# 64 small identity products in TensorE's program, and an opening re-ordered around them, in a delta-rule attention and MLP kernel

## The chip, the cores and the metric

One core of a Trainium2 chip. The metric is the device time of one execution in microseconds; several runs of the same kernel are given by their median. Lower is better.

## What is computed

Four sequences, eight heads, 768 tokens, 48 features per head, all fp32. The attention block runs the delta rule token by token; its output, 3072 x 384, goes through an MLP with 2048 hidden units and a hard swish.

```python
k_n = k / (norm(k, axis=-1) + 1e-06)
state = zeros((B, H, D, D))
for t in range(S):
    y[:, :, t] = einsum('bhd,bhde->bhe', q[:, :, t], state)
    v_old = einsum('bhde,bhd->bhe', state, k_n[:, :, t])
    state = state + beta[:, :, t] * einsum('bhd,bhe->bhde', k_n[:, :, t], v[:, :, t] - v_old)
x = y.transpose(0, 2, 1, 3).reshape(B * S, H * D)
h = x @ w_in
out = (h * clip(h + 3, 0, 6) / 6) @ w_out
```

The inputs also hold weights in a 64-bit type, which the kernel converts on the chip.

## The kernel before

**Chunks.** Tokens are taken in 24 chunks of 32 for all four sequences at once (128 partitions). Within a chunk the recurrence is solved in closed form: a lower triangular system of 32 unknowns per head and sequence is inverted. Chunk 0 is inverted by a chain of small products (`product`); chunks 1 to 4 (group 1) are inverted together on VectorE by elimination of the two 16 x 16 halves (`halves_of`: a transposition L469, pairs of steps L730 and L735, a transposition back L473), and then each of these chunks joins its two halves by two products on TensorE (`join`, L684 with the names pi1 and pi2). Later groups are inverted wholly on VectorE.

**What a chunk needs, step by step.** `prep`: the keys are scaled on GpSimd (kb, L510), keys and queries are turned by four transpositions each on TensorE (pt, L524), and ScalarE sets the results aside (KQ, L532); TensorE then forms the products of keys and queries (sc, L547), and VectorE masks them into L and LB (L558). `chain`: the products with the state (ks, L806), R on VectorE (L901, L909), the product with the inverse (pz, L827), set aside by ScalarE (R, L927), the change of the state (su, L938; added by VectorE, L956), and the output: the product py (L827), set aside as y (L861 for chunk 0), turned on TensorE (yt, L873) and set aside as xT (L877). Chunk 0 needs no ks.

**The MLP.** xT of two chunks makes a block of 256 tokens. Block 0 is multiplied chunk by chunk with w_in (ph, L994; a "chunk of ph" below is one of the 16 column tiles of 128 hidden units, three products of 128 x 128). ScalarE takes a relu of each (g, L1001), VectorE multiplies (g, L1004). The down products (po) follow, and later blocks are multiplied by schemes with fewer products (L1066, L1226), which make up most of the time.

**The weights.** They arrive in 16 pieces of 768 KB through SP's queue (L331). For each piece ScalarE makes four passes (the scale steps, L356) and VectorE three (the convert steps L378, L383 and L389). Two buffers of scales alternate: the scale steps of a piece wait for the last convert step of the piece two before it. The bytes of a piece are loaded once the first passes over an earlier piece in the same place are done.

**Order.** Each engine works strictly through its own list. For the opening, the lists come from a table of words, ORDER, each of which lets one generator make its next step: `a` a scale step, `c` a convert step, `w` a weight load, `k`, `q`, `v` loads, `pN` a step of chunk N's prep, `hN` one of its chain, `yN` one of its output, `i1` a step of the elimination of group 1, `xN` a step of chunk N's product or join, `ua` a chunk of ph, `ra` its relu, `ga` its product. From chunk 5 on a planner spreads the steps.

**The opening's joint.** Before the change TensorE's list around the first join reads: nine products of ph (three chunks), ks of chunk 1, eighteen products of ph, pi1, six products of ph, pi2, three products of ph, pz of chunk 1. The first product of TensorE's program is the transposition of chunk 0's keys, which waits for GpSimd.

Of the kernel before, what the change touches and what calls it, by code (L numbers as in the profile page):

```python
# [22 lines left out]
k*2 B*3 k*2 n0 k*2 z B s*2 n0*6 k*2 q*2 n1 q n1 q w k p0 z*3 k n1*2 k*2 n1*2 z p0*2 s k p0*3 a k a  # L23
m0 a n2 m1 p0 x0*2 w q x0 n1 x0*3 c*2 n2 a k s p1*2 a s*2 k q s*2 x0 n2 k*2 c x0 n2 x0 w q a*4 q p1
n2 k*2 a x0 m2 p1 c*2 p1 n2*3 b1 q b0 s p1 x0 q w x0 n2 q*2 c*3 x0 n4 k p1 k p2*2 x0*2 a*2 c a*2 q*3
a*2 w v p3*2 q x0 q n4 p2*2 c p2 v c n4*2 a*3 z v n4 c a m3 v c p2 n4*2 q p2 k c b2 h0 c h0 w a*2 h0
p4*2 a*2 m4 p3 q*4 h0 q k w p4*2 c*5 v*2 p3 k p3*3 k*2 p4*2 v*2 p4 m6 k a w a w i1*3 k i1*7 a i1*2 a
i1*2 v i1*2 k b3 k y0 c y0*3 ua*2 ra*2 i1*3 w v ga v a*3 i1*2 ua i1 h1 i1 q w ua ra ua i1 ra*2 ga i1
k ua a*2 ra ga i1 ga ua ra ua ra i1 ga i1*4 ua ga n5 x1*2 k x1 c a ra v a*2 ga x2 k*2 ga*2 ua*2 x1
ra*2 x1*2 ua h1*2 n5 k ga c ra ga*2 h1 c y1*2 ua ra w ga ua ra x2 n5 ga y1*2 ua ra ga h1 v*3 n5*2 k  # L30
y1*2 ua a ra x2 ub*2 a n5 rb*2 h1 x3 ga c*2 v W a h2 y2 gb ub rb gb x2 gb ub*2 n5*2 b4 rb n5 x2*2 h2
gb rb gb m5 a n5*2 y2 ub rb gb v c q*2 v q*5 n5 ub n5 rb gb h2 c h2 q ub y2 h2 y2 rb ub p5 b5 rb
gb*2 a*2 x3 p5 ub y2*2 k p5*2 h2 rb h3 p5 gb h3 ub*2 q rb gb rb gb ub a x3 p6 v c x4 x3 rb gb ub p7
rb gb y3 c*2 v c p7*2 y3 v p7*2 b6 x3 q x3 ub p6 h3 a p6 c p5*2 rb gb k m7 w p6 h3 u p6 k*2 q*3 a*2
y3 a p6 c y3 v y3*2 u n9 v k q a c a c*2 u*2 ru gu w k a*2 c a*2 x4 c*2 ru p7 a gu k u a*2 p7 p6 m8
u*3 a k u*2 k h3 w ru*2 a*2 gu*2 x4 c*2 x4 k c*2 a p8 k a*2 u ru k h3 u*2 h4 ru a b8 gu k gu y4 p8*3
u h4 k*2 c q k*9 q u p8*2 x4 k ru k*2 gu k c n9 q u q*2 p8 k*2 b7 n9*2 i2 u x4 q i2*2 q ub ru gu u
rb gb i2*2 h4*2 u*2 i2 ru i2*6 y4 i2 gu i2*7 u i2 ru gu i2 u*3 ru i2*4 gu ru i2*2 v i2 c gu u*3 a u
ru c i2 u*2 i2 gu i2*3 q i2*5 y4 h4 n9 i2 e*2 n9*2 i2*4 q i2 y4 e n9 u ru i2*3 u i2 ru*2 gu h4 u n9
i2*2 u i2 e i2*6 y4 u k n9*3 u gu i2 y4 n9 i2 p9 q i2*2 gu  # L40
"""


# [1 line left out]
def kernel(  # L45
# [21 lines left out]
    nc = tc.nc  # L67
    B, H, S, D = q.shape
    DM, FF = moe_w_in.shape
    C, DP = 32, 64  # L70
# [11 lines left out]
    G0 = 1  # L82
# [12 lines left out]
    def rows(b):  # L95
        return slice(C * b, C * b + C)
# [4 lines left out]
    def group(t):  # L101
        return (0, t) if t < G0 else ((t - G0) // GS + 1, (t - G0) % GS)
# [34 lines left out]
    def needs(*what):  # L137
        assert past.issuperset(what), (what, set(what) - past)
# [70 lines left out]
    ident = const.tile([128, 128], FP32, name="ident")  # L209
# [87 lines left out]
    def pad(t):  # L297
        return [f"pad{t}"] if t < NBKB else []
# [195 lines left out]
    def scaled(t):  # L494
# [7 lines left out]
        past.add(("bkb", t))  # L502
        yield

    def prep(t, whole=True):

        g, i = group(t)
        kb, qb = kbufs[t % NKB], qbufs[t % NQB]
        needs(*([("bkb", t - NKB)] if t >= NKB else []), *(pad(t) if t < NKB and t else []))
        nc.gpsimd.tensor_tensor(  # L510
            out=kb[:, :, 0:D], in0=kfs[g][:, i],
            in1=invs.pop(t).unsqueeze(2).to_broadcast([P, H, D]), op=ALU.mult,
        )
        past.add(("kb", t))
        yield

        for j, src in enumerate((kb, qb)):
            if j == 1:
                needs(("q", t))
                past.add(("qT", t))  # L520
            ring("pm", NPM, ("pt", t, j))
            pt = psM.tile([128, NP, P], FP32, name="pt", tag=slot["pm"])
            for p in range(NP):
                nc.tensor.transpose(  # L524
                    pt[:, p, :], src[:, 2 * p : 2 * p + 2].rearrange("p e w -> p (e w)"), ident[:]
                )
            yield 1
            if j == 0:
                ring("KQ", NKQ, ("KQ", t))
                KQ = work.tile([128, NP * B // 2, 4, C], FP32, name="KQ", bufs=NKQ)  # L530
            read(("pt", t, j))
            nc.scalar.activation(  # L532
                out=KQ[:, :, 0:4:3, :] if j == 0 else KQ[:, :, 1:3, :],
                in_=pt[:].rearrange("q p (x y c) -> q (p x) y c", y=2, c=C), func=ACTF.Copy,
            )
            if whole and j == 0:
                drain(mask(t))
            yield
# [26 lines left out]
        if whole:  # L565
            drain(scaled(t))
        yield
# [98 lines left out]
    def join(t):  # L666
# [11 lines left out]
        def times(name, m, k):  # L678
            ring("pm", NPM, (name, t))
            ps = psM.tile([P, H, HC], FP32, name="pi", tag=slot["pm"])  # L680
            for h in range(H):
                for b in range(B):
                    r = slice(C * b, C * b + k)
                    nc.tensor.matmul(  # L684
                        ps[rows(b), h, :], lhsT=m[r, h, :], rhs=LT[r, h, HC:C],
                        start=True, stop=True, skip_group_check=True,
                        tile_position=(C * b, C * b),
                    )
            return ps
# [6 lines left out]
        ps = times("pi1", T, HC)  # L696
# [10 lines left out]
        ps = times("pi2", T2, C)  # L707
# [638 lines left out]
    def drain(gen):  # L1346
        for _ in gen:
            pass
# [53 lines left out]
    def early_norms(t):  # L1402
# [7 lines left out]
        a=scales(), c=rest, w=pieces(), q=queries(), v=values(), B=betas(), k=keys(), z=settings(), s=more_settings(),  # L1410
        ua=up(0, 0), ub=up(0, 1), u=mlp_units(),
# [40 lines left out]
    with tc.manual_schedule():  # L1452
        for word in ORDER.split():
            word, _, n = word.partition("*")
# [14 lines left out]
        for t in range(LS, N):  # L1469
            g, i = group(t)  # L1470
# [94 lines left out]
```

## Time and profile before

| | us |
|---|---|
| median of 3 runs | 663.66 (663.46 to 663.9) |
| the profiled execution | 662.06 |
| its span, first to last instruction | 660.3 |
| TensorE busy in it | 632.5 (96%) |
| TensorE weight loads | 569.2 (86%) |
| VectorE busy | 499.2 (76%) |
| ScalarE busy | 282.3 (43%) |
| GpSimd busy | 225.1 (34%) |

How to read it: PE is TensorE, PEld its weight loads, DVE VectorE, ACT ScalarE, POOL GpSimd, SP SyncE, which issues most loads and stores. A group "pi L684 x64" stands for 32 products in fp32: each is two weight loads and two passes over the array. A transposition of 128 x 128 is one of each. The page cuts the span into 40 slices of 16.5 us; the opening spoken of here takes the first four. In the timelines each row has its start and its length in us, the engine, the line, the operation with its tiles and shapes, the count, and in brackets the idle time ahead of it with what ended it; "issue" is idle time that no semaphore explains. In the tables by stretch, "3.62 (x201)" is a busy time and a count, and the column PEclk is the share of TensorE's clock that was granted.

### The profile page before, as it was taken

Reading aid. Unit: us, or ns where it says so; the run is one execution under the profiler, and the core shown is the slowest. Engines: PE = TensorE matmul, PEld = TensorE weight load, DVE = VectorE, ACT = ScalarE, POOL = GpSimd, SP = SyncE. Lnnn points to the kernel's source line nnn. Section 1 sums busy time; section 2 is a strip of 40 time slices with the busy share of each in tenths; the row PEclk is TensorE's granted clock in tenths of the full one; section 3 lists DMA queues with packets and bytes.
Section 4 is the critical chain, followed back from the end, with each engine's and each line's share of the span. In section 5 each row is a group of like instructions: output and inputs, shape, how many; then the busy total and the mean of one; then the engine's idle time right before and its main releaser. Section 6 shows DMA issues by size and latency. Waiting matters only on the chain.

```text
span 660.3 us, 26640 instructions
## 1 busy us (share of the span) xinstructions
PE 632.5 (96%) x11640; PEld 569.2 (86%) x11640; DVE 499.2 (76%) x1170; ACT 282.3 (43%) x548; POOL 225.1 (34%) x352
## 2 busy tenths in 40 slices
PE   2768999999999999999999999999999999999997
PEld 2658987776689989999999999999999999999997
DVE  5899877798657988758988848979658998456354
ACT  5887689332243154154154244244244144153250
POOL 6531022003661353553254354164051242331430
PEclk9998999999999999999999999999999999999999
DMA  7888346202040030041030030020020020000000
GB/s 174 204 198 235 77 102 164 51 25 43 9 87 18 3 74 3 3 90 22 3 74 3 2 74 3 2 63 2 3 50 2 3 49 3 23 18 2 26 1 24
DMA packets 88692, 33.28 MB, mean 50 GB/s; under 512 B 80224, under 2 KB 83424, under 8 KB 88576
## 3 DMA queue, kind: packets, MB, share of 16 engines
q1 hardware_dynamic: 88224, 31.29, 20.8%
q8 instruction: 91, 1.49, 0.9%
q10 hardware_dynamic: 352, 0.30, 0.2%
q14 instruction: 25, 0.20, 0.1%
HBM read 26.84 MB, written 4.72 MB: 48 GB/s over the span
## 4 chain that ended last, share of the span: by engine, by line
PE 91%; DVE 3%; DMA 2%; SPq 1%; ACT 1%; issue 1%; DVEq 0%
PE po L1226 28%; PE ph L1066 27%; PE ph L994 9%; PE po L1162 6%; PE ks L806 4%; PE su L938 3%; PE pt L524 3%; PE pz L827 3%; PE py L827 3%; PE sc L547 2%; PE yt L873 1%; DMA spare<-in_moe_w_in_dram 1%; PE pi L684 1%; DMA w_out<-in_moe_w_in_dram 1%; SPq L168 1%
## 5 line engine op out<-in xcount | busy, mean ns | idle before, releaser
L1066 PE MATMUL ph<-xT,w_in 128*128 128x128 f32 (+1 forms) x720 | 156.8, 321 | 0.0
L1030 POOL TENSOR_TENSOR g<-g 128x256 f32<-128x256 f32 (+1 forms) x144 | 88.6, 616 | 104.7 <-ACT g L1080 99.1
L1066 PEld LDWEIGHTS ph<-xT,w_in 128*128 128x128 f32 x720 | 116.8, 191 | 6.7
L1226 PE MATMUL po<-w_out,g 128*128 128x192 f32 x640 | 110.6, 326 | 0.0
L1226 PEld LDWEIGHTS po<-w_out,g 128*128 128x128 f32 x640 | 104.6, 190 | 0.5
L1080 ACT ACTIVATE g<-ph 128x512 f32<-128x512 f32 x72 | 43.1, 598 | 105.1 <-PE ph L1066 105.1
L1226 PE MATMUL po<-spare,g 128*128 128x192 f32 x480 | 86.7, 332 | 0.0
L1226 PEld LDWEIGHTS po<-spare,g 128*128 128x128 f32 x480 | 77.2, 190 | 1.8
L994 PE MATMUL ph<-xT,w_in 128*128 128x128 f32 (+1 forms) x384 | 72.0, 338 | 0.6 <-ACT xT L877 0.6
L1236 POOL TENSOR_TENSOR o<-o,u 128x192 f32<-128x192 f32 x18 | 13.3, 739 | 163.8 <-ACT o L1233 86.6
L994 PEld LDWEIGHTS ph<-xT,w_in 128*128 128x128 f32 x384 | 59.6, 195 | 7.7 <-ACT xT L877 0.8
L1093 DVE TENSOR_TENSOR g<-ph,g 128x256 f32<-128x256 f32 x72 | 30.2, 419 | 46.8 <-PE ph L1066 33.5
L759 DVE TENSOR_TENSOR pr<-A 128x30 f32<-128x30 f32 (+9 forms) x150 | 57.3, 382 | 3.3
L1212 DVE TENSOR_TENSOR g<-g 128x512 f32<-128x512 f32 x80 | 56.1, 722 | 3.5 <-PE po L1226 3.5
L1113 DVE SCALAR_TENSOR_TENSOR g<-o,g 128x512 f32<-128x512 f32 x72 | 52.6, 730 | 7.8 <-ACT o L1110 7.7
L764 DVE TENSOR_TENSOR A<-A,pr 128x30 f32<-128x30 f32 (+9 forms) x150 | 55.1, 367 | 3.3
L1110 ACT ACTIVATE o<-g,halves 128x512 f32<-128x512 f32 x72 | 52.2, 725 | 11.3 <-DVE g L1113 8.4
L1066 PE MATMUL ph<-beta_tok,sums_in 128*128 128x128 f32 x288 | 55.9, 275 | 0.0
L356 ACT ACTIVATE spare<-spare,places 128x768 uint16<-128x768 uint16 (+1 forms) x56 | 52.8, 947 | 3.2 <-DMA kf<-in_k_dram 1.6
L1233 ACT ACTIVATE o<-po 128x192 f32<-128x192 f32 x40 | 13.3, 332 | 82.7 <-PE po L1226 79.2
L510 POOL TENSOR_TENSOR kb<-kf,inv 128x384 f32<-128x384 f32 x24 | 21.7, 907 | 75.5 <-issue 43.1
L1162 PE MATMUL po<-w_out,g 128*128 128x384 f32 x128 | 45.4, 490 | 0.0
(141 smaller groups left out, 1019.1 us busy)
## 6 DMA issues: line engine op xcount, KB each, us to landing
kf<-in_k_dram SPq DMA_DIRECT2D x96, 48.0 KB, 2.6
qb<-in_q_dram SPq DMA_DIRECT2D x96, 48.0 KB, 2.4
vf<-in_v_dram SPq DMA_DIRECT2D x96, 48.0 KB, 2.1
out_dram<-o SPq DMA_DIRECT2D x90, 48.0 KB, 1.6
spare<-in_moe_w_in_dram SPq DMA_DIRECT2D x4, 768.0 KB, 6.6
w_out<-in_moe_w_in_dram SPq DMA_DIRECT2D x4, 768.0 KB, 6.1
w_out<-in_moe_w_out_dram SPq DMA_DIRECT2D x4, 768.0 KB, 5.8
spare<-in_moe_w_out_dram SPq DMA_DIRECT2D x4, 768.0 KB, 5.2
```

The costliest lines, as they stand in the source:

```text
L356: nc.scalar.activation(out=z, in_=z if n else d.bitcast(I16)[:, :, :, 3], func=func, bias=places[:, n : n + 1], scale=scale,)
L759: nc.vector.tensor_tensor(out=pv, in0=A[:, j + 1 :, j].unsqueeze(2).to_broadcast([n, w, j]), in1=A[:, j, 0:j].unsqueeze(1).to_broadcast([n ...
L764: nc.vector.tensor_tensor(out=A[:, j + 1 :, 0:j], in0=A[:, j + 1 :, 0:j], in1=pv, op=ALU.subtract)
L994: nc.tensor.matmul(ph[:, cols], lhsT=w_in[:, s, f * 128 : (f + 1) * 128], rhs=xT[:, s, cols], start=(s == 0), stop=(s == NKT - 1),)
L1030: nc.gpsimd.tensor_tensor(out=out, in0=a, in1=b, op=op)
L1066: nc.tensor.matmul(ph[:, n], lhsT=w, rhs=x, start=start, stop=stop, skip_group_check=True)
L1080: nc.scalar.activation(out=gt, in_=ph[:], func=ACTF.Copy)
L1110: nc.scalar.activation(out=r, in_=g, func=ACTF.Relu, bias=half, scale=1.0 / 6.0)
L1113: nc.vector.scalar_tensor_tensor(out=g, in0=r, scalar=1.0, in1=g, op0=ALU.min, op1=ALU.mult)
L1162: nc.tensor.matmul(pos[c][:], lhsT=gs[blk, f // 2][:, f % 2, c * P : (c + 1) * P], rhs=w_out[:, f, :], start=(f == 0), stop=(f == NFC - 1),)
L1212: nc.vector.tensor_tensor(out=A(f, *out, 4), in0=A(f, *a, 4), in1=A(f, *b, 4), op=op)
L1226: nc.tensor.matmul(ps[n][:], lhsT=A(f - f % 2, *a)[:, f % 2], rhs=b[:, f], start=(f == 0), stop=(f == HF - 1),)
```

## The change

Small products of an identity are added: each takes 16 rows and 32 columns of `ident` as weights and 16 columns of it as data, and writes into a tile that the following products overwrite. 58 of them stand at the head of TensorE's program, ahead of the first transposition; six stand ahead of the first join's pi1. The table ORDER is changed in its middle; the same words stand in another order there, and before and behind that part it is as it was. No other line changes.

```diff
+    def small_ones(ps, n):
+        for i in range(n):
+            b = i % B
+            nc.tensor.matmul(
+                ps[rows(b), 0, 0 : C // 2], lhsT=ident[C * b : C * b + C // 2, 0:C],
+                rhs=ident[C * b : C * b + C // 2, 0 : C // 2],
+                start=True, stop=True, skip_group_check=True, tile_position=(C * b, C * b),
+            )
+
+    LEAD, TRAIL = 58, 64 - 58
...
             pt = psM.tile([128, NP, P], FP32, name="pt", tag=slot["pm"])
+            if (t, j) == (0, 0):
+                small_ones(pt, LEAD)
...
             ps = psM.tile([P, H, HC], FP32, name="pi", tag=slot["pm"])
+            if (t, name) == (G0, "pi1"):
+                small_ones(ps, TRAIL)
```

The part of ORDER that differs, from the same word to the same word, before and after:

```diff
-a*3 z v n4 c a m3 v c p2 n4*2 q p2 k c b2 h0 c h0 w a*2 h0 p4*2 a*2 m4 p3 q*4 h0 q k w p4*2 c*5 v*2
-p3 k p3*3 k*2 p4*2 v*2 p4 m6 k a w a w i1*3 k i1*7 a i1*2 a i1*2 v i1*2 k b3 k y0 c y0*3 ua*2 ra*2
-i1*3 w v ga v a*3 i1*2 ua i1 h1 i1 q w ua ra ua i1 ra*2 ga i1 k ua a*2 ra ga i1 ga ua ra ua ra i1 ga
-i1*4 ua ga n5 x1*2 k x1 c a ra v a*2 ga x2 k*2 ga*2 ua*2 x1 ra*2 x1*2 ua h1*2
+a*2 z v n4 c m3 v c p2 n4*2 q p2 k c b2 h0*2 p3 a w p3*2 h0 a h0 p4*2 p3 a m4 q*4 c p3 q k w p4*2 c
+p4*2 c v*2 p4 k*3 v*2 a m6 k y0 a y0 a*2 w a w i1*3 k i1*7 a i1*2 a i1*2 c v i1*2 k b3 k y0*2 ua*2
+ra*2 i1*3 w v ga v a*3 i1*2 ua i1 h1 i1 q w ua ra ua i1 ra*2 ga i1 k ua a ra ga i1 ga ua ra ua ra i1
+ga i1 ua i1*2 ra ga ua ra ga i1 n5 x1*2 ga c*2 k ua x1 c a c a v a*2 x2 k*2 ga x1 ra x1*2 ua h1*2
```

On the engines this reads as follows. GpSimd's and SP's lists are as they were. TensorE: the transposition of chunk 3's queries moves ahead of su of chunk 0, sc of chunk 3 ahead of the transposition of chunk 4's queries; two chunks of ph (six products) that lay between pi1 and pi2 now stand ahead of pi1, with the six small products between them and it. ScalarE: the eviction R of chunk 0 stands two scale steps sooner; the KQ evictions of chunks 3 and 4 stand between scale steps, not behind eight of them; y of chunk 0 stands ahead of five scale steps, and xT behind these five; five relus are taken in a row ahead of the join, where some scale steps lay between them; ahead of the first join's X eviction (L710) now stand the four scale steps of one piece together and one relu. VectorE: L and LB of chunk 3 come sooner; three convert steps leave the place ahead of L469; two more products g stand ahead of L473; between L694 and L698 of the first join stand one g, the convert steps L378, L383, L389 and L378, and one g, where L378 and three g stood.

More of the change, by code (lines that the diff above doesn't have):

```diff
@@ L25 @@
 n2 k*2 a x0 m2 p1 c*2 p1 n2*3 b1 q b0 s p1 x0 q w x0 n2 q*2 c*3 x0 n4 k p1 k p2*2 x0*2 a*2 c a*2 q*3
[L26 to L39, printed above, removed]
@@ L40 @@
-i2*2 u i2 e i2*6 y4 u k n9*3 u gu i2 y4 n9 i2 p9 q i2*2 gu
+a*2 w v p3*2 q x0 q n4 p2*2 c p2 v c n4*2 a*2 z v n4 c m3 v c p2 n4*2 q p2 k c b2 h0*2 p3 a w p3*2
+h0 a h0 p4*2 p3 a m4 q*4 c p3 q k w p4*2 c p4*2 c v*2 p4 k*3 v*2 a m6 k y0 a y0 a*2 w a w i1*3 k
+i1*7 a i1*2 a i1*2 c v i1*2 k b3 k y0*2 ua*2 ra*2 i1*3 w v ga v a*3 i1*2 ua i1 h1 i1 q w ua ra ua i1
+ra*2 ga i1 k ua a ra ga i1 ga ua ra ua ra i1 ga i1 ua i1*2 ra ga ua ra ga i1 n5 x1*2 ga c*2 k ua x1
+c a c a v a*2 x2 k*2 ga x1 ra x1*2 ua h1*2 n5 k ga c ra ga*2 h1 c y1*2 ua ra w ga ua ra x2 n5 ga
@@ new lines @@
+y1*2 ua ra ga h1 v*3 n5*2 k y1*2 ua a ra x2 ub*2 a n5 rb*2 h1 x3 ga c*2 v W a h2 y2 gb ub rb gb x2
+gb ub*2 n5*2 b4 rb n5 x2*2 h2 gb rb gb m5 a n5*2 y2 ub rb gb v c q*2 v q*5 n5 ub n5 rb gb h2 c h2 q
+ub y2 h2 y2 rb ub p5 b5 rb gb*2 a*2 x3 p5 ub y2*2 k p5*2 h2 rb h3 p5 gb h3 ub*2 q rb gb rb gb ub a
+x3 p6 v c x4 x3 rb gb ub p7 rb gb y3 c*2 v c p7*2 y3 v p7*2 b6 x3 q x3 ub p6 h3 a p6 c p5*2 rb gb k
+m7 w p6 h3 u p6 k*2 q*3 a*2 y3 a p6 c y3 v y3*2 u n9 v k q a c a c*2 u*2 ru gu w k a*2 c a*2 x4 c*2
@@ L41 @@
+ru p7 a gu k u a*2 p7 p6 m8 u*3 a k u*2 k h3 w ru*2 a*2 gu*2 x4 c*2 x4 k c*2 a p8 k a*2 u ru k h3
+u*2 h4 ru a b8 gu k gu y4 p8*3 u h4 k*2 c q k*9 q u p8*2 x4 k ru k*2 gu k c n9 q u q*2 p8 k*2 b7
+n9*2 i2 u x4 q i2*2 q ub ru gu u rb gb i2*2 h4*2 u*2 i2 ru i2*6 y4 i2 gu i2*7 u i2 ru gu i2 u*3 ru
+i2*4 gu ru i2*2 v i2 c gu u*3 a u ru c i2 u*2 i2 gu i2*3 q i2*5 y4 h4 n9 i2 e*2 n9*2 i2*4 q i2 y4 e
+n9 u ru i2*3 u i2 ru*2 gu h4 u n9 i2*2 u i2 e i2*6 y4 u k n9*3 u gu i2 y4 n9 i2 p9 q i2*2 gu
 """
```

## The prediction

> **What bounds the kernel now.** First the page's slices, for where TensorE is not yet full; then the busy time by stretch; then, for the opening, the timelines of TensorE, ScalarE and VectorE one above the other.
>
> ```profile
> PE   2768999999999999999999999999999999999997
> PEclk9998999999999999999999999999999999999999
> ```
>
> PE is full from the fifth slice (66 us) on. By stretch (busy us and count of PE, PEld, DVE, ACT, POOL, then PEclk):
>
> ```profile
> 45.00:51.80 6.80, 3.62 (x201) 3.16 (x202) 6.49 (x15) 5.26 (x8) 2.26 (x5) 1.00 0.84 260
> 51.80:55.20 3.40, 3.40 (x38) 3.18 (x40) 3.12 (x11) 2.18 (x4) 0.00 (x0) 0.50 1.05 288
> 62.00:70.00 8.00, 8.00 (x293) 7.30 (x294) 7.41 (x21) 5.21 (x12) 2.15 (x4) 1.00 0.28 71
> ```
>
> From 62 us PE never waits (8.00 of 8.00), and no later stretch has it wait until its last 3 us. So the change is worth what it does to the moment at which PE, with a given list of products behind it, becomes full. The two orders are the same again from the first join's last step on, so I measure that moment at pz of token chunk 1 (L827), which starts at 64.95 now; the list behind it is the same before and after. The half clock after the thin stretch (0.50) comes back below.
>
> PE in the opening:
>
> ```profile
> 39.29 1.27 PE L938 MATMUL su<-R,sums_in 32*64 32x48 f32 x61 [1.75 <-ACT R L927]
> 41.31 0.44 PE L938 MATMUL su<-R,sums_in 32*64 32x48 f32 x3 [0.75 <-issue]
> 46.63 0.88 PE L827 MATMUL py<-R,LB 32*32 32x48 f32 x64
> 49.92 0.55 PE L873 MATMUL yt<-ident,y 128*128 128x128 f32 x3 [2.41 <-ACT y L861]
> 51.05 3.55 PE L994 MATMUL ph<-xT,w_in 128*128 128x128 f32 x18 [0.58 <-ACT xT L877]
> 61.24 0.72 PE L684 MATMUL pi<-X,sums_in 16*32 16x16 f32 x64 [0.94 <-DVE sums_in L694]
> ```
>
> PE waits for ScalarE's evictions (R, y, xT), for VectorE's transposition (L694), and once, inside su, for nothing that has a semaphore. ScalarE and VectorE:
>
> ```profile
> 35.99 2.88 ACT L356 ACTIVATE spare<-spare,places 128x768 uint16<-128x768 uint16 x3
> 38.77 0.47 ACT L927 ACTIVATE R<-pz 128x384 f32<-128x384 f32 x1
> 45.51 3.98 ACT L356 ACTIVATE spare<-spare,places 128x768 uint16<-128x768 int16 x4
> 49.40 0.47 ACT L861 ACTIVATE y<-py 128x384 f32<-128x384 f32 x1
> 50.51 0.49 ACT L877 ACTIVATE xT<-yt 128x384 f32<-128x384 f32 x1 [0.64 <-PE yt L873]
> 64.22 0.28 ACT L710 ACTIVATE X<-pi 128x128 f32<-128x128 f32 x1
> ```
>
> ```profile
> 47.70 1.93 DVE L469 STREAM_TRANSPOSE A<-L 128x1024 f32<-128x1024 f32 x1
> 58.71 2.00 DVE L473 STREAM_TRANSPOSE X<-A 128x1024 f32<-128x1024 f32 x1
> 60.74 0.45 DVE L694 STREAM_TRANSPOSE sums_in<-X 128x256 f32<-128x256 f32 x1
> 62.15 0.28 DVE L698 TENSOR_TENSOR sums_in<-pi,corner 128x128 f32<-128x128 f32 x1
> ```
>
> Between 34.3 and 51 us ScalarE is nearly full: twelve scale steps (L356, 0.97 each from start to start) and eight evictions. xT comes behind all of them, and PE's own work (ph) starts behind xT.
>
> **The code's borders.** The page's third part has queue q8 with 91 packets and 1.49 MB: 16 KB each, and 2 x 11640 PE instructions of 64 bytes are 1.49 MB, so a packet is 256 of PE's instructions. A small product is four of them (32 products of L684 stand as x64 MATMUL, with as many weight loads): 64 products are one packet, and behind the sixth small product of the trailing part every border lies where it lay. In between, 58 x 4 = 232 instructions push the borders: each stands 24 instructions behind the place of the one before it. Counted out: the border five instructions before the end of su goes to some 20 instructions into pz (36.03); the next comes at the start of sc of chunk 3; the one after that some 15 instructions before the end of sc of chunk 4. In the trace the packet for the su border starts at 38.23, lands at 39.81, and PE resumes at 41.31: about 5.3 us after PE had entered the packet before, 1.50 after landing. The next one lands at 44.68 and is entered at 46.30. So the wait in su is late code, and I expect the same pace: border in pz at 36.2, sc of chunk 3 not before 36.2 + 5.2 = 41.4, the last products of sc of chunk 4 not before 41.4 + 5.0 = 46.4. The su wait (0.75) does go; two others come, and the second ends where the old order had its sc as well (46.70). The Trainium skill, page "Runtime: NRT & Kernel Launch", section "Instruction fetch mechanics", speaks of the same 16 KiB blocks but calls the crossing mostly hidden. By that page the sum below would be about 1.2 us smaller; the 0.75 us in su speaks against it here.
>
> **The 64 products.** Nearest row: the first join's 32, 0.72 us, same shape. 58 at full clock are 1.3 us, at the half clock that the opening's transposes show (0.9 us for four, 0.44 later) 2.6. They need only ident, ready at 1.90, and end by 4.5; the next product waits for the keys until 8.08. Cost nothing; without that cover 2.6. Nor do I give them an effect on the clock: bursts of small products as long (1.1 us of L596, pauses of 2 us) leave it at half until 45 us in the trace. The six cost 0.14 at the join and are covered by VectorE's delay there.
>
> **ScalarE's order.** R moves ahead of two scale steps: it can start when pz ends (37.5, 1.2 us sooner), with 0.6 us of new idle time. The keys' and queries' evictions go between single scales; y goes ahead of its scales. But the number of scale steps ahead of xT is still twelve, and now five stand between y and xT. y waits for py, py for the late code: 46.4 + 0.1 + py 0.88 + y 0.47 = 47.9 (now 49.87). yt is then ready at 48.4 and xT waits for 5 x 0.97: it ends at 47.9 + 4.85 + 0.49 = 53.2, now 51.00. ph starts 2.2 us later. ScalarE's idle time that pays for this: 0.6 before R, about 1 before the queries, near 2 before y, against 0.9 now.
>
> **VectorE's order.** Three convert steps (L378, L383, L389: 0.57, 0.97, 0.97) leave the place ahead of L469; A can start when sc of chunk 4 ends plus two products, 46.5 + 0.8 = 47.3 (now 47.70). The elimination takes 11.0 from there, so X (L473) could start at 58.3. But seven products g (L1004) now stand ahead of it, five before, and each needs a finished ph chunk: 7 x 0.77 + ks 1.08 = 6.5, plus 1.2 for the half clock (three chunks took 3.48, 2.3 at full clock), plus relu and product 0.65, minus 0.3 that the modelled ends overlap: 53.2 + 8.05 = 61.3. X ends at 63.3, L694 at 63.75 (now 61.19).
>
> Behind L694 stand now g, L378, L383, L389, L378, and only then L698: 0.2 + 0.57 + 0.97 + 0.97 = 2.7 to the end of L389. For that conversion waits the first of four scale steps on ScalarE (the buffer of two pieces earlier), 1.00 + 2.88, and queued behind those four, ahead of pz, is the first join's X eviction (L710), with one relu (0.37). 63.75 + 2.7 + 3.9 + 0.35 = 70.7; now 64.22. PE is meanwhile idle (the two chunks that lay between the join's products are ahead of them): pz at 70.7 + 0.33 = 71.05, now 64.95. **Sum: 6.1 us later.** The queues of SP and POOL keep their order; SP's loads that wait for a scale start up to 6 us later, all for use as much later.
>
> The profiled execution took 662.06, its span 660.3; the median of the runs is 663.66, 1.60 above. 662.06 + 6.1 = 668.2 for such an execution, and 663.66 + 6.1 = **669.8** for the median.
>
> **Rivals.** *Code never late:* if the borders cost nothing, sc of chunk 4 ends near 45 and all behind it moves by 1.2 to 2.5: +3.5 to +4.9, 667 to 668.6; at the most, with the clock full as well, ScalarE's own sum (xT not before 49.5) leaves +1.7, 665.4. The page named above would have it so. For it: no border after 62 us shows a wait. Against: the one at 41.31.
>
> *Half clock again:* PE idles some 4.5 us ahead of ph and most of 65 to 71. A stretch with 3.62 of 6.80 busy was followed by 3.4 us at 0.50. If the second idle time brings another, 3.4 us of full PE cost 0.9 to 1.7 more, and a second one ahead of X 1.2: +7.3 to +8.9, up to 672.5. The Trainium skill, "TensorE: Matmul & The Clock Gate", Part 1, has a free-running window of 3413 ns and two states; the row at 51.80 agrees in length and ratio.
>
> *Faster:* the opening is bound by VectorE's elimination, and the early evictions bring it forward. The su wait (0.75), R's 1.2 and the 0.94 ahead of the first join would then all be saved, about 2 us after overlap: 661.7. It needs the conversions and scales ahead of L698 and L710 to find cover: the tail from L694 to L710 grows from 3.0 to 7.0, so L694 would have to end by 57.2, 4.0 sooner than now. Even with A at 45.0 and 11.0 behind it, it ends at 58.5. I see no way there.
>
> **Chances.** Forecast (+4.9 to +7.3) 0.55; code never late 0.17; half clock again 0.16; faster 0.08; no change 0.04. 665.4 to 672.5 holds the first three nearly whole. A measurement tells 0.2%, 1.3 us. Faster 0.08, same 0.04, slower 0.88.
>
> **What would show it.** In the changed profile: su without its "issue" wait; sc of chunk 3 near 41.4 with an issue wait ahead; five L356 between y and xT; ph from about 53; L698 some 3 us behind L694; four L356 ahead of L710; pz of chunk 1 near 71. Wrong it is if xT ends by 51, or if L710 runs before 66.

## The result

The kernel after takes 671.85 us (median of 4 runs, 670.84 to 672.65), the kernel before 663.56 (median of 4, 662.48 to 663.9). The ratio of after to before is 1.0126, with a 95% interval of 1.0111 to 1.0141: slower by 8.3 us. The forecast was 669.8, with a range of 665.4 to 672.5.

The profiled execution of after took 672.65 us, its span is 670.8 us (before: 662.06 and 660.3). The page's slices for TensorE and for its granted clock:

```profile
PE   3667899999999999999999999999999999999997
PEclk9777799999999999999999999999999999999999
```

TensorE is full from the sixth slice on, one later than before. In the clock row slices two to five are below full, where before only the fourth was; but by the rows of the timelines, before ran its opening at half clock too, up to about 45 us, where its clock row shows 9. Its pz of chunk 0 takes 1.50 us, and py, with the same shape and count, 0.88 at 46.63:

```profile
36.03 1.50 PE L827 MATMUL pz<-vf,X 32*32 32x48 f32 x64
```

What is new is how much half clock there is behind 45 us: before had a mean share of 0.90 from 45 to 62 us. By stretch (busy us and count of PE, PEld, DVE, ACT, POOL, then PEclk, the share of the DMA engines and GB/s):

```profile
45.00:62.00 17.00, 11.67 (x233) 10.41 (x234) 11.57 (x36) 11.96 (x19) 2.26 (x5) 0.58 0.84 230
62.00:70.00 8.00, 4.24 (x107) 3.95 (x105) 7.32 (x17) 4.12 (x9) 0.00 (x0) 0.96 0.15 43
70.00:80.00 10.00, 9.78 (x287) 8.97 (x288) 7.19 (x17) 5.75 (x13) 2.15 (x4) 0.69 0.26 75
```

From 62 to 70 us, where TensorE had no gap before, it works 4.24 of 8.00. The clock averages 0.58 from 45 to 62 us and 0.69 from 70 to 80 us. TensorE's timeline shows the single waits:

```profile
39.25 0.84 PE L953 MATMUL su<-R,sums_in 32*64 32x48 f32 x60 [0.80 <-DVE LB L571]
42.29 1.17 PE L560 MATMUL sc<-KQ 64*32 64x64 f32 x64 [1.61 <-DVE w_in L389]
46.78 0.43 PE L560 MATMUL sc<-KQ 64*32 64x64 f32 x5 [0.45 <-issue]
54.22 4.21 PE L1009 MATMUL ph<-xT,w_in 128*128 128x128 f32 x18 [4.07 <-ACT xT L892]
70.03 1.05 PE L699 MATMUL pi<-X,sums_in 32*32 32x16 f32 x64 [3.14 <-DVE sums_in L717]
72.85 1.50 PE L842 MATMUL pz<-R,X 32*32 32x48 f32 x64 [0.19 <-ACT X L725]
110.06 2.21 PE L1009 MATMUL ph<-xT,w_in 128*128 128x256 f32 x9 [0.68 <-issue]
```

The wait inside su without a releaser is gone. A program border now makes the last five instructions of sc of chunk 4 late (0.45 at 46.78), and the 1.61 ahead of sc of chunk 3 is one too: the page names L389 as the releaser, but that convert step has nothing to do with sc; the packet of the program landed 1.72 us ahead of that product. In other kernels below the row at the same border names ScalarE's L356 (0.77 us, with the join's weight steps behind X) or "issue" (0.25 us, in the first fill). ph waits 4.07 us for xT, pi2 waits 3.14 us for VectorE, and pz of chunk 1 starts at 72.85 instead of 64.95. ScalarE and VectorE:

```profile
48.71 0.49 ACT L876 ACTIVATE y<-py 128x384 f32<-128x384 f32 x1 [1.77 <-PE py L842]
49.10 4.70 ACT L356 ACTIVATE spare<-spare,places 128x768 uint16<-128x768 uint16 x5
53.70 0.47 ACT L892 ACTIVATE xT<-yt 128x384 f32<-128x384 f32 x1
68.47 1.01 ACT L356 ACTIVATE spare<-w_out,places 128x768 uint16<-128x768 int16 x1 [2.94 <-DVE w_in L389]
69.51 2.87 ACT L356 ACTIVATE spare<-spare,places 128x768 uint16<-128x768 uint16 x3
72.53 0.27 ACT L725 ACTIVATE X<-pi 128x128 f32<-128x128 f32 x1
```

```profile
48.00 1.94 DVE L469 STREAM_TRANSPOSE A<-L 128x1024 f32<-128x1024 f32 x1
60.66 0.29 DVE L1019 SCALAR_TENSOR_TENSOR g<-g,ph 128x128 f32<-128x128 f32 x1 [2.41 <-ACT g L1016]
63.35 1.98 DVE L473 STREAM_TRANSPOSE X<-A 128x1024 f32<-128x1024 f32 x1
65.36 0.45 DVE L709 STREAM_TRANSPOSE sums_in<-X 128x256 f32<-128x256 f32 x1
67.48 0.96 DVE L389 SCALAR_TENSOR_TENSOR w_in<-spare 128x768 f32<-128x768 f32 x1
69.14 0.28 DVE L713 TENSOR_TENSOR sums_in<-pi,corner 128x128 f32<-128x128 f32 x1
```

Five scale steps stand between y and xT; VectorE reaches the last elimination steps early and then waits 2.41 us for a relu of ph; L389 ends at 68.44 and releases the four scale steps that stand ahead of the eviction of X.

### The profile page after: what moved, and what is told of

Its sections match the earlier page's. It is cut to its first block, busy times and chain, and to the rows that moved or that the text cites. A ratio compares the mean times of both kernels' runs of the same rounds, so it can differ in the third digit from the quotient of the medians.

```text
span 670.8 us, 26895 instructions
## 1 busy us (share of the span) xinstructions
PE 637.1 (95%) x11768; PEld 572.3 (85%) x11768; DVE 499.7 (74%) x1170; ACT 281.0 (42%) x548; POOL 224.0 (33%) x352
## 4 chain that ended last, share of the span: by engine, by line
PE 92%; ACT 3%; DVE 3%; issue 1%; SPq 0%; DMA 0%; POOL 0%; ACTq 0%; DVEq 0%
PE po L1241 28%; PE ph L1081 27%; PE ph L1009 10%; PE po L1177 6%; PE ks L821 4%; PE pt L537 3%; PE py L842 3%; PE pz L842 3%; PE sc L560 3%; PE su L953 3%; ACT spare L356 2%; PE yt L888 1%; PE pi L699 1%; DVE w_in L389 1%; DVE spare L378 0%
## 5 line engine op out<-in xcount | busy, mean ns | idle before, releaser
L1081 PEld LDWEIGHTS ph<-xT,w_in 128*128 128x128 f32 x720 | 116.9, 191 | 6.9 <-issue 0.3
L1009 PEld LDWEIGHTS ph<-xT,w_in 128*128 128x128 f32 x384 | 61.4, 202 | 12.6 <-ACT xT L892 4.5
L356 ACT ACTIVATE spare<-spare,places 128x768 uint16<-128x768 uint16 (+1 forms) x56 | 52.3, 941 | 3.2 <-DVE LB L571 2.1
```

Of the source, the lines that this page charges most:

```text
L356: nc.scalar.activation(out=z, in_=z if n else d.bitcast(I16)[:, :, :, 3], func=func, bias=places[:, n : n + 1], scale=scale,)
L1009: nc.tensor.matmul(ph[:, cols], lhsT=w_in[:, s, f * 128 : (f + 1) * 128], rhs=xT[:, s, cols], start=(s == 0), stop=(s == NKT - 1),)
L1081: nc.tensor.matmul(ph[:, n], lhsT=w, rhs=x, start=start, stop=stop, skip_group_check=True)
```

## The experiments

Two theories were to be told apart. The chain theory: the opening is a chain through y, xT, ph, X and pz of chunk 1, each link of which can be read from a row, and what is late at pz is late at the end. Its rivals: the late program, the half clock, or the products themselves are what costs, and the order only rides along. Each kernel's ratio is to runs of before on the same chip. The edits are against the kernel after.

This table has, from one profiled execution of each, the starts of y, X (L473 of group 1) and pz of chunk 1, the end of xT, the time from X to pz, the span, and what of the span lies behind the start of pz.

| | y | xT ends | X | pz | X to pz | span | behind pz |
|---|---|---|---|---|---|---|---|
| before | 49.40 | 51.00 | 58.71 | 64.95 | 6.24 | 660.3 | 595.4 |
| after | 48.71 | 54.17 | 63.35 | 72.85 | 9.50 | 670.8 | 598.0 |
| old order, products | 50.86 | 52.82 | 61.40 | 67.64 | 6.24 | 663.1 | 595.5 |
| new order, no products | 47.06 | 52.53 | 61.12 | 70.62 | 9.50 | 667.4 | 596.8 |
| new front, old join | 46.87 | 52.32 | 62.22 | 68.44 | 6.22 | 664.3 | 595.9 |
| old front, join with one convert step | 50.03 | 51.63 | 60.62 | 67.10 | 6.48 | 663.9 | 596.8 |
| old front, new join | 49.75 | 51.68 | 61.10 | 70.59 | 9.49 | 668.1 | 597.5 |
| join's weight steps behind X | 48.08 | 53.55 | 62.87 | 68.87 | 6.00 | 669.1 | 600.2 |
| xT directly behind y | 48.23 | 49.85 | 60.13 | 69.61 | 9.48 | 667.6 | 598.0 |
| both of these | 53.54 | 55.51 | 65.81 | 72.70 | 6.89 | 671.6 | 598.9 |
| products 48 and 16 | 47.14 | 52.59 | 61.16 | 70.65 | 9.49 | 668.7 | 598.1 |
| fill ahead of ph, 58 | 47.52 | 53.00 | 60.26 | 69.76 | 9.50 | 670.5 | 600.7 |
| fill ahead of ph, 55 | 46.89 | 52.36 | 59.60 | 69.10 | 9.50 | 666.8 | 597.7 |

**The products alone: the order of before, 64 products.**

```diff
 ORDER = """          # all words as in the kernel before
 ...
     LEAD, TRAIL = 58, 64 - 58
```

> The 64 small products with the old ORDER. Theory 1 (the order alone costs the 8.3 us, by ScalarE and VectorE standing idle and their steps coming late): no change, within 0.2% (-0.5 to +0.8 us): the wait in su goes, another border falls into the old sc of chunks 3 and 4, which waits for its evictions anyway. Theory 2 (late code at the moved borders costs): +1.2 to +2 us. The products themselves end before 4.5 us in either.

Measured: 664.15 us, ratio 1.0026 (1.0012 to 1.0040). The products by themselves cost about 1.7 us; they were not free. That is the figure of theory 2, and a late border is there: pz of chunk 0 waits 0.85 us for its program at 37.46. But part of the delay is older. It is visible at the very start of the run, in ScalarE's squares of the keys (L407) and its first eviction in chunk 0's inversion. First this kernel, then the new order without products:

```profile
4.84 0.52 ACT L407 ACTIVATE sq<-kf 128x384 f32<-128x384 f32 x1 [2.54 <-DMA kf<-in_k_dram]
7.56 0.52 ACT L407 ACTIVATE sq<-kf 128x384 f32<-128x384 f32 x1 [1.28 <-DMA kf<-in_k_dram]
17.19 0.36 ACT L637 ACTIVATE sums_in<-pi 128x256 f32<-128x256 f32 x1
```

```profile
4.99 0.52 ACT L407 ACTIVATE sq<-kf 128x384 f32<-128x384 f32 x1 [2.69 <-DMA kf<-in_k_dram]
6.57 0.52 ACT L407 ACTIVATE sq<-kf 128x384 f32<-128x384 f32 x1
15.13 0.36 ACT L637 ACTIVATE sums_in<-pi 128x256 f32<-128x256 f32 x1
```

The first square is no later, the second waits for its keys. In all twelve profiles with products it starts at 7.19 to 7.91 and L637 at 16.20 to 17.19; in the two without, at 6.48 and 6.57, and 15.52 and 15.13. Of the queues in the first 12 us the kernel after shows

```profile
q8 instruction: 1, 0.02, 0.5%
```

and before shows no packet of q8 there. The 58 products carry TensorE over the border of its first block at 3.2 us, and a packet of the program (started between 4.0 and 4.9 us) moves among the first loads of keys. That it is this packet which holds up the keys is inferred from the times; it was not tested by itself. Nor are the late start, the late border and the half clock (to 58.28 us, in before to 55.22) told apart in what this kernel lost.

**The order alone: no products.**

```diff
-    LEAD, TRAIL = 58, 64 - 58
+    LEAD, TRAIL = 0, 0 - 0
```

> The new ORDER without any small product. Theory 1: the whole loss, +7.5 to +9 us. Theory 2 (the moved borders): +6 to +7, with sc of chunk 3 at once behind its eviction. In the profile: five scale steps between y and xT as before, xT ends near 53, and the first join's X eviction near 72.

Measured: 669.02 us, ratio 1.0108 (1.0081 to 1.0134). So most of the loss belongs to the order: about 7.2 us, between the two theories' figures. Without products the late program is in su again (1.85 us at 40.03), xT ends 1.64 sooner than in after, X starts 2.23 sooner, and X to pz takes the same 9.50.

**The front half, and the join, apart.** The first kernel has the new front, with the three convert steps put back ahead of the elimination, and the old join; the second has the old front and a join in which one convert step stands between pi1 and pi2; the third has the old front less three convert steps, and the new join whole. All keep the 64 products.

```diff
 # new front, old join
-y0 a*2 w a w i1*3 k
+y0 a*2 w a w c*3 i1*3 k
 ...
-k ua a ra ga i1 ga ua ra ua ra i1 ga i1 ua i1*2 ra ga ua ra ga i1 n5 x1*2 ga c*2 k ua x1 c a c a v a*2
-x2 k*2 ga x1 ra x1*2 ua
+k ua a*2 ra ga i1 ga ua ra ua ra i1 ga i1*4 ua ga n5 x1*2 k x1 c a ra v a*2 ga x2 k*2 ga*2 ua*2 x1
+ra*2 x1*2 ua
```

> All 64 products and the front half of the new ORDER (R, keys, queries and y sooner), with the three convert steps put back ahead of the elimination and the old joint (pi1, two chunks of ph, pi2). Theory 1: +3 to +4.5 us: xT still ends near 53 behind five scale steps, the elimination starts late because the third of the three convert steps waits for its scales; the join itself costs nothing more. A rival that puts the whole loss on the join's converts and scales gives no change here.

Measured: 666.79 us, ratio 1.0074 (1.0049 to 1.0100), about 4.9 us; with this interval it fits the +3 to +4.5. As expected, the third convert step waits for its scales (L389, 1.35 us at 48.21), and A starts at 51.30 instead of 48.00. The rival with no change is out.

```diff
 # old front, join with one convert step
-x1*2 ga c*2 k ua x1 c a c a v a*2 x2 k*2 ga x1 ra x1*2
+x1*2 ga k ua x1 a c a v a*2 x2 k*2 ga x1 ra x1*2
```

> All 64 products, the old front half, and the new joint: two chunks of ph ahead of pi1, one convert step (not four) between the join's two products. Theory 1: +1.5 to +2.5 us: two more products g stand ahead of the transposition back, and nothing covers pi2's wait. With front_only that is well under the 8.3 us of both: the rest comes of the two together (the three convert steps that move into the join, and the scales behind them). A rival in which the halves simply add gives front_only + back_only = 8.3.

Measured: 665.57 us, ratio 1.0048 (1.0031 to 1.0065), about 3.2 us, more than the +1.5 to +2.5. The two come to 1.22%, near the 1.26% of after, which is what the rival "the halves simply add" gave. But both hold the 0.26% of the products, so this sum counts them twice; and the first kernel's late A is no part of after. So the sum is no evidence that the halves add.

```diff
 # old front less three convert steps, new join
-p4*2 c*5 v*2                    (the old front)
+p4*2 c*2 v*2
```

> The 64 identity products and the order of before, except that the join has the order of after with all three more convert steps, which stood ahead of the elimination, between the join's first and second product group. Nothing is left out. It does the joint part of the change alone; the run with the old opening and one convert step there came to 1.0048 of before, and the one with the old order to 1.0026. Chain theory (VectorE goes through convert steps between the two product groups, and ScalarE's scale steps stand ahead of the eviction of X): the transpose A starts about 2 us sooner than in the old order, but ScalarE's and VectorE's work between transpose X and the start of pz grows from 6.2 us to 9.2 to 9.6 us; pz starts at 69.5 to 71, and the time is 1.008 to 1.011 of before. Rival (what A gains pays for the join): 1.002 to 1.005. Rival (late code and the clock of the new opening are what costs): the same 1.002 to 1.005, with no wait of over 1 us ahead of the join's second product group.

Measured: 669.46 us, ratio 1.0104 (1.0078 to 1.0130); pz at 70.59, X to pz 9.49. This is what the chain theory said; the 1.002 to 1.005 of both rivals lies outside the interval. From the second kernel this one differs by the three convert steps alone, which stand in the join here and ahead of the elimination there: 1.0104 against 1.0048. The three together: X to pz is 6.22 to 6.48 without the moved convert steps and 9.48 to 9.50 with them in every kernel of the table whose join is new. The new join by itself, on top of the products, costs 0.0104 - 0.0026, about 5.2 us: 3.25 of them between X and pz, the rest behind pz (597.5 against 595.5) where the idle join lets the clock fall. The timeline of TensorE in the third kernel:

```profile
67.78 1.05 PE L699 MATMUL pi<-X,sums_in 32*32 32x16 f32 x64 [3.14 <-DVE sums_in L717]
70.59 1.50 PE L842 MATMUL pz<-R,X 32*32 32x48 f32 x64 [0.18 <-ACT X L725]
72.02 2.64 PE L1009 MATMUL ph<-xT,w_in 128*128 128x128 f32 x12
78.89 1.60 PE L1009 MATMUL ph<-xT,w_in 128*128 128x128 f32 x12
```

The same wait of 3.14 as in after, to the hundredth, and behind pz twelve ph that take 2.64 at a clock of a half for most of them, against 1.60 at the full clock.

**xT directly behind y.**

```diff
-m6 k y0 a y0 a*2 w a w i1*3 k
+m6 k y0 a y0*3 a*2 w a w i1*3 k
 ...
-k b3 k y0*2 ua*2
+k b3 k ua*2
```

> The kernel after with one stretch of ORDER changed: the transpose yt and the eviction xT stand directly behind the eviction of y, as they did in the kernel before, with the five scale steps behind them. Nothing is left out. Chain theory: xT ends at about 49.8 to 50.5 in place of 54.17, ph starts about 4 us sooner, the wait of 2.41 us that VectorE has at 58.3 for g is gone or under 0.7 us, X ends 2 to 2.5 us sooner (about 63.0 in place of 65.33), pz starts at 70 to 71, and the time falls by 1.5 to 2.8 us against the kernel after: 669.0 to 670.5. Rival (VectorE's own run of 63 steps behind the transpose A sets X, and ph is hidden in it): X moves by under 0.7 us and the time stays at 671 to 672.5. Rival (half clock): ph sooner only makes TensorE idle later, the clock stays at 0.974 to 0.98 and the gain is under 1 us.

Measured: 669.05 us, ratio 1.0063 (1.0039 to 1.0087), clear of after's interval: 0.63%, or about 4.2 us, of after's loss comes from the five scale steps between y and xT. The point lies above the 1.5 to 2.8 that were expected, but the two intervals together allow 2.3 us as well, and the two profiled spans differ by 3.2. xT ends at 49.85, VectorE's wait for g at the end of the elimination falls from 2.41 to 0.28 us at most, and X starts at 60.13 instead of 63.35; the elimination behind A (L469, at 48.15) sets it then. X to pz is unchanged. With the same join the old front, less its three convert steps, gave 1.0104 and this one 1.0063: once xT is back behind y, the early evictions of the new front seem to gain something (the intervals still overlap).

**The join's convert and scale steps behind the eviction of X.**

```diff
-x1*2 ga c*2 k ua x1 c a c a v a*2 x2 k*2 ga x1 ra x1*2 ua h1*2 n5 k ga c ra ga*2 h1 c y1*2 ua
+x1*2 ga k ua x1 v x2 k*2 ga x1 ra x1*2 ua h1*2 n5 c*2 k ga c ra ga*2 c h1 c y1*2 a*4 c ua
```

> The kernel after with one stretch of ORDER changed: the join's four convert steps on VectorE and the four scale steps on ScalarE, which stand between pi1 and the eviction of X, stand behind that eviction instead. Nothing is left out. Chain theory (the start of chunk 1's pz sets the rest: span = that start + 595.4 us, + half of the half-clock time that is left behind it): in the kernel after VectorE needs 4.17 us from the end of the join's first transpose (65.81) to the end of its second (69.98), against 1.84 us in the run with the old order and the 64 products (63.88 to 65.72), and ScalarE sets X aside at 72.53 instead of 1.2 us behind that; so pz should start 2.3 to 4 us sooner, at 69 to 70.5, and the time fall by 2 to 3.5 us against the kernel after, to 668.0 to 670.0. Rival (the convert steps are needed by then anyway, and wait elsewhere): pz comes sooner, but the later products wait for the weights, and the time stays at 671 to 672.5. Rival (half clock is the whole cost): no change, 671 to 672.5, with the same clock of 0.974 to 0.982.

Measured: 670.99 us, ratio 1.0101 (1.0082 to 1.0121); against after's 1.0126 (1.0111 to 1.0141) not clearly better. TensorE:

```profile
67.35 0.73 PE L699 MATMUL pi<-X,sums_in 32*32 32x16 f32 x64 [0.95 <-DVE sums_in L717]
68.87 1.56 PE L842 MATMUL pz<-R,X 32*32 32x48 f32 x64
72.03 2.93 PE L1009 MATMUL ph<-xT,w_in 128*128 128x128 f32 x12 [1.59 <-DVE w_in L389]
```

pz is 4 us sooner, X to pz falls to 6.00, and then ph waits 1.59 us for the weights that the moved convert steps make, at half clock until 75.86. Of 4 us, 2.3 are given back behind pz (600.2 against 598.0). The rival was half right: the weights are the next thing late, so those convert steps cannot simply go behind the join either. Their better place was ahead of the elimination, where before had them (1.0048 against 1.0104 above).

**Both of these together** (the join keeps one convert step).

```diff
-x1*2 ga c*2 k ua x1 c a c a v a*2 x2 k*2 ga x1 ra x1*2 ua h1*2 n5 k ga c ra ga*2 h1 c y1*2 ua
+x1*2 ga c k ua x1 v x2 k*2 ga x1 ra x1*2 ua h1*2 n5 c k ga c ra ga*2 c h1 a c a y1*2 a*2 c ua
```

> The kernel after with both stretches of ORDER mended: yt and xT directly behind the eviction of y, and the join's convert and scale steps behind the eviction of X but for one convert step. Nothing is left out. Alone the first brought 1.0063 of before and the second 1.0101, where after has 1.0126. Chain theory: the two add, pz starts at 65.5 to 67.5, the work that was moved behind X costs a wait for weights of 1 to 2 us later, and the time is 1.002 to 1.005 of before. Rival (the weights bound the stretch behind the join, so that an earlier pz only waits longer): the gain of the second falls away, 1.006 to 1.008, with a wait of 2.5 us or more at the convert step L389 for TensorE's ph.

Measured: 667.89 us, ratio 1.0081 (1.0055 to 1.0106). The two did not add: 1.002 to 1.005 was expected of that, and the ratio lies just above the rival's 1.006 to 1.008. About 5.4 us of the loss are left with both steps mended, so these two are not the whole of it; the products' 1.7 us and the late weights are in the rest, which no run takes apart. The profiled execution was the longest of its six (673.27), with 3.11 us of late program in sc of chunk 4, which makes its y late; from X on it shows the same picture, X to pz 6.89, and then a wait of 2.09 us at 78.89 for w_in L389 (the rival had named 2.5 or more).

**Where the products stand: 48 at the head, 16 ahead of the join; and then 48 small ones with nine whole identity products ahead of ph and seven ahead of pi2.**

```diff
-    LEAD, TRAIL = 58, 64 - 58
+    LEAD, TRAIL = 48, 64 - 48
```

> The kernel after with 48 of the 64 identity products at the head of the program and 16 ahead of the first join, in place of 58 and 6. Nothing is left out. The borders between blocks of 256 TensorE instructions move by 20 instructions between the two places. Chain theory: no difference by more than 1 us against the kernel after, 670.8 to 672.8, as the 16 products ahead of pi1 stand in TensorE's idle time. Code theory (a border of the program in sc of chunk 3 or 4 sets the opening): the borders fall 20 instructions later in the program there, which saves at most the 1.5 us and 0.45 us that TensorE waits at 42.29 and 46.78 in the kernel after: 669.9 to 671.5. It is also what the next kernel is compared with.

```diff
-    LEAD, TRAIL = 58, 64 - 58
+    LEAD, TRAIL = 48, 48 - 48
+    def full_ones(ps, n):
+        for _ in range(n):
+            nc.tensor.matmul(ps, lhsT=ident[:], rhs=ident[:], start=True, stop=True, skip_group_check=True)
...
+            if (t, name) == (G0, "pi2"):
+                full_ones(ps[:].rearrange("p h c -> p (h c)"), 7)
...
+            if (blk, f, half_of) == (0, 0, 0):
+                full_ones(ph[:, cols], 9)
```

> The run before this with other fill: 48 small products at the head, none ahead of the first join; instead nine products of the whole 128x128 identity ahead of the first ph and seven ahead of pi2, so that the number of TensorE instructions, and the borders of its program behind them, stay as they were. They write into tiles that the products behind them overwrite. Nothing is left out. Clock theory (TensorE idle in the windows around 42 to 59 and 66 to 76 us lets the granted clock fall to half, and the half clock is worth 2 us or more of the time): TensorE is busy 1 to 2 us more in those windows, the granted clock of the run is at 0.980 or more, and the time falls by 1 to 3 us against the 48/16 kernel. Chain theory (half clock counts only where a product on the chain runs): the nine products cost nothing ahead of ph as TensorE waits there for xT, the seven at most 0.9 us ahead of pi2, and the time is within -1.5 and +0.5 us of the 48/16 kernel, by whether the second half-clock stretch ends sooner.

Measured: 673.41 us, ratio 1.0144 (1.0104 to 1.0184), above what either theory gave, and 669.60 us, ratio 1.0086 (1.0054 to 1.0117; five executions, and a sixth of 678.02 that is not in these figures). The intervals overlap and the executions scatter (670.4 to 678.5 of the first), so this pair settles nothing about the clock. Ten small products are 40 instructions, not 20, so the borders between the two places moved by 40. The second kernel is not in the table: its X to pz is 10.65, because the seven whole products, which start at 71.01, hold up pi2 until 73.28. One thing that can make such a scatter was seen in its profiled execution (674.12): in sc of chunk 3 TensorE stood still for its program.

```profile
45.56 0.93 PE L564 MATMUL sc<-KQ 64*32 64x64 f32 x44 [3.87 <-issue]
50.63 1.20 PE L848 MATMUL py<-R,LB 32*32 32x48 f32 x49 [0.76 <-issue]
```

The stretch from 40 to 46 us has the DMA engines wholly taken (share 1.02 in the table by stretch), and the packet that usually starts 1 to 2.5 us after the border before it started 6.6 us after it.

**The clock ahead of ph by itself.** Nine whole identity products ahead of the first ph, none ahead of the join, 58 small ones at the head; then the same with 55, so that the program behind the join is as long as that of after.

```diff
-    LEAD, TRAIL = 58, 64 - 58
+    LEAD, TRAIL = 58, 58 - 58          (second kernel: 55, 55 - 55)
...
+            if (blk, f, half_of) == (0, 0, 0):
+                full_ones(ph[:, cols], 9)
```

> The kernel after with the six products ahead of the first join left out and nine products of the whole 128x128 identity ahead of the first ph, where TensorE waited 4.07 us for xT; they write into the tile that ph overwrites. The program up to there is that of after, and behind the join it is three products longer. Nothing is left out. Clock theory (the half clock from 42.05 to 59.11 us is worth about 2 us, as the 18 products of ph took 4.21 us at half clock and 36 took 4.29 us at full): TensorE is busy from about 50 on, the clock is full again by about 56, the wait of 2.41 us that VectorE has for g shrinks to under 1 us, pz starts 1 to 2 us sooner, at 71 to 72, and the time is 1.009 to 1.011 of before. Rival (the five scale steps ahead of xT are the whole cost there, the clock only rides along): the clock recovers, but X ends within 0.5 us of where it ended in after (65.33), and the time stays at 1.0115 to 1.0135.

Measured: 672.75 us, ratio 1.0153 (1.0126 to 1.0180). The clock is full from 51.92 on instead of 59.11, pz starts at 69.76 instead of 72.85, and yet the span is 670.5:

```profile
48.45 3.80 PE L518 MATMUL ph<-ident 128*128 128x128 f32 x18
53.06 2.27 PE L1015 MATMUL ph<-xT,w_in 128*128 128x128 f32 x18 [0.81 <-ACT xT L896]
69.76 1.50 PE L846 MATMUL pz<-R,X 32*32 32x48 f32 x64 [0.20 <-ACT X L729]
105.94 2.37 PE L1183 MATMUL po<-w_out,g 128*128 128x384 f32 x4 [1.72 <-issue]
```

The 18 ph instructions that took 4.21 us in after take 2.27. From the end of xT to X it is 7.26 us instead of 9.18. But at 105.94 TensorE waits 1.72 us for its program, and the clock is at half from 106.54 to 109.95, where after lost 0.68. Both theories stated for this run missed its time: neither had that wait.

> The kernel with nine whole identity products ahead of the first ph again, with 55 small ones at the head of the program in place of 58, so that behind the join the program is as long as that of after. Nothing is left out. The kernel with 58 ran at 1.0153 of before, though its pz started at 69.76 in place of 72.85: TensorE waited 1.72 us for its program at 105.94, ahead of the second expert's ph, and the clock fell to half from 106.54 to 109.95. Theory (three products shift the border of the program from the third ph of that stretch, where after waited 0.68 us at 110.06, onto an earlier place with less time since the border before): with 55 the wait is 0.7 us or less again, there is no half clock behind 100 us, pz starts at 69.5 to 71, and the time is 1.006 to 1.010 of before. Rival (the wait at 106 us comes from the load on the queues in that run, not from the border's place; or a stretch that is reached sooner has its program later): the wait and the half clock stay, 1.0115 to 1.016.

Measured: 669.33 us, ratio 1.0116 (1.0095 to 1.0137). In its profile there is no half clock behind 72.55 and no wait of 1.7; from xT to X it is 7.24, pz starts at 69.10 and the span is 666.8. By the profile the theory holds; its 1.006 to 1.010 was missed, though the interval reaches into it, and the gain over after cannot be told from nothing, as the executions reach from 667.9 to 671.4. What is shown is the clock's price in this link, 1.9 us; that it can be had for good is not.

## Why the prediction was right, and what was mis-sized

The sign and the mechanism were right, the size was short: +6.1 forecast, +8.3 by the medians. That is above the +4.9 to +7.3 that had the chance of 0.55. The two profiled spans differ by 10.5, because the execution of after was the longest of its four and that of before lies 1.6 below its median; the steps below add up to this 10.5, 7.9 ahead of pz and 2.6 behind it.

- *Code borders.* The wait in su is gone and two others came, in the places that were counted out: sc of chunk 3 at 42.29 (not before 41.4 was forecast), the end of sc of chunk 4 at 46.78 (46.4). They are not what sets the loss: the new order without products, whose borders lie as before, loses about 7.2 us, and its interval overlaps that of after. It has a late border of its own, though (1.85 us in su), so no run shows the new order without one. The rival "code never late" falls with these rows.
- *ScalarE.* Five scale steps lie between y and xT, as forecast; xT ends at 54.17 instead of 53.2. y ends 1.3 later than forecast, at 49.20 instead of 47.9, and the way from there to xT is 0.4 shorter. Of the 1.3, 0.62 is py, put at 0.88 and measured at 1.50, at half clock. The rest lies in sc of chunks 3 and 4, behind an opening that is late from its start: sc of chunk 2 starts at 35.70 instead of 34.92. How much of this 0.78 reaches y is not shown. It comes from the first failed term: the 58 products at nothing. Their 1.78 us lie free indeed (they end at 3.7, the next product starts at 8.40), but the row that showed their cover was TensorE's alone; the keys come about 1 us later behind it.
- *VectorE.* From the end of xT to X 8.1 was forecast and 9.18 measured. The forecast had the half clock for three chunks of ph, 1.2; it lasted from 42.05 to 59.11, and the fill shows 1.9 for it. The other 0.4 is not taken apart here. X starts at 63.35, not 61.3.
- *The join.* From X to pz 9.75 was forecast and 9.50 measured, in after and in six other kernels: VectorE's convert steps and ScalarE's four scale steps in series, as said.
- *Behind pz* nothing was forecast but the list as it was; 2.6 more came. At half clock lay 3.33 us (72.85 to 76.18), half of which is 1.7, and the program was late by 0.68 at 110.06. In the table the same sum holds: with 595.4 behind pz, half of the half-clock time left and the later waits, the new order without products should have 596.7 and has 596.8, the one with xT behind y 598.0 and has 598.0. The other kernels of the table come within half a microsecond of this sum, if half clock is counted only while TensorE works.

So the rival "half clock again" came true on top of the forecast, inside of what it gave (+7.3 to +8.9). The forecast had counted the second stretch of half clock as a chance of 0.16, where it was the rule: every profile with the new join has one that starts between pi1 and the first products behind pz, and no profile with the old join has any there. The Trainium skill, page "TensorE: Matmul & The Clock Gate", Part 1, has the window of 3.4 us and a phase that differs from run to run; the trace agrees, its clock changes only in steps of 3.41 us. An idle stretch need not fill such a window. TensorE worked 0.85 of the 3.41 us ahead of the second half clock in after, 1.81 in the kernel with the old front and one convert step in the join, and 2.46, with small products, in the one with the weight steps behind X; in before the stretch from 58.63 to 62.04, 2.47 of 3.41 at work, was followed by full clock. Whoever had put such a thin stretch, as the forecast had it from 65 to 71 us, beside the one at 45 to 51.80 would have had the clock in the sum.

The rivals "faster" and "no change" are excluded. No kernel tried beat the kernel before; the nearest, the products with the old order, is 0.26% above it.

## What to carry to other kernels

Moving weight-preparing steps out of one engine's crowded stretch is worth only what the next engine's list lets through: write down, for each moved step, what then stands ahead of the next eviction on its engine, and look for the place where two engines wait for each other in series, as between the two halves of the join. Count every stretch of idle TensorE that a new order makes twice, once for itself and once for the products behind it at half clock. And instructions added to an idle engine need not be free: the 58 small products took 1.78 us of TensorE's idle time and, with the six at the join, cost 0.26%, though TensorE's own row showed them covered.

## What the runs showed of the hardware

- *The program can be late by much more than a packet's length.* In this opening a block's packet mostly starts 1 to 2.5 us after TensorE has entered the block before and takes 0.9 to 2.1 us, and TensorE never went on sooner than 1.2 us after it had landed. That made waits of 0.2 to 1.85 us, and twice more, 3.11 and 3.87, where the packet itself started 4.2 and 6.6 us after the border. The Trainium skill, page "Runtime: NRT & Kernel Launch", section "Instruction fetch mechanics", has the next block fetched while the current one runs, and calls the crossing mostly hidden. The first agrees with the order of packets and borders seen here. The second fits most crossings, as no border of before behind 62 us shows a wait; it does not fit the waits named above.
- *Three products can decide where the program is late, 40 us later.* With 67 products the wait was 1.72 us at 105.94, with 64 it was 0.68 at 110.06 in after and at most 0.2 us there in the second fill (one profile each).
- *The profile's clock can read full where the products run at half.* In before the clock row shows 9 in the first three slices, and the stretch from 0 to 45 us has a mean of 1.00, while 32 products of one shape (x64) take 1.50 us at 36.03 and 0.88 at 46.63. So the mean clock of an execution is no measure of its half clock: of fifty later executions of the kernel before the one at 0.971 took 663.10 us, the one at 1.0 took 663.26, and the shortest (660.68) was at 0.989. What the half clock costs was read above from single links of the chain: ahead of X and behind pz.
